# A hint at the head of the program for the branch over a fallback path

## The chip, the cores and the metric

The kernel runs on one core of a Trainium2 chip. A core has a matrix engine (TensorE, PE in the profile; its weight loads are shown as PEld), a vector engine (VectorE, DVE), an activation engine (ScalarE, ACT), a general engine (GpSimd, POOL) and a control engine (SyncE, SP). Each executes its own stream of instructions, in order; the streams meet only at semaphores. DMA queues move data between the device's memory and the core's own memories, and two of the queues in the profile, 8 and 14, move instructions.

The metric is the device time of one execution in microseconds. The time before the change is 607.65 us, the median of three runs (606.86, 607.65 and 607.78).

## The reference

The computation is an attention over normalised queries and keys, followed by a residual two-layer network. For 8 batches, 12 heads, 448 positions and a head width of 64:

```python
q_n, k_n = rmsnorm(q, g_q), rmsnorm(k, g_k)
scores = scale * np.matmul(q_n, k_n.transpose(0, 1, 3, 2))
scores = scores - np.max(scores, axis=-1, keepdims=True)
attn = np.exp(scores)
attn = attn / (np.sum(attn, axis=-1, keepdims=True) + 1e-09)
attn_out = np.matmul(attn, v)

x = attn_out.transpose(0, 2, 1, 3).reshape(8, 448, 768)
xn = (x - mean(x)) / np.sqrt(var(x) + 1e-06) * g_ln
out = x + np.maximum(xn @ w_ch1, 0.0) @ w_ch2
```

The weights w_ch1 and w_ch2 are 768 x 3072 and 3072 x 768. Inputs and output are 32-bit floats in the device's memory.

## The kernel before

The kernel has two versions of the whole computation. The fast one takes shortcuts: the exponential takes a constant offset (EXP_BIAS) in place of each row's maximum, and matmuls run in 16-bit floats. The general one, `_general`, takes the maximum of every row and goes through the batches in a loop, for inputs on which the shortcuts would lose accuracy. The fast version runs always. A test at its end decides whether the general one runs after it and overwrites the output. With the inputs measured here it does not run.

The fast version first does the attention of batch 0, in an order of work written out by hand (the table ORDER). Then `run_rest` walks through the batches. For each it lays out the network's work in chunks (`mlp_chunks`: 24 "up" chunks of six matmuls with 512 columns, L652, and then "down" chunks of six matmuls, L668), and between them it puts the steps of the next batch's attention. For the last batch nothing is left to put between: `run_rest` emits its chunks one after the other, and after the third it calls `flag`. The last down chunks are those of the fourth token tile, and the last 384 columns of that tile are done as two groups of 192. After each group VectorE adds the residual (L672), and `store` sends the rows out (L712), one half on SyncE's queue and one on ScalarE's.

The order is manual on all engines but VectorE in this second part; VectorE's order there is set by the framework's scheduler.

`flag` counts on VectorE how many of the recorded quantities lie inside safe bounds, sums over partitions with one matmul, and writes 0 or 1 to a one-element tile. Then, in the main function, `values_load` (L935) loads that element into a register of every engine (TENSOR_LOAD in the profile), and `tc.If` (L936) becomes one compare-and-branch on every engine:

```python
    val = nc.values_load(sh.flag[0:1, 0:1], min_val=0, max_val=1)
    with tc.If(val > 0):
        _general(tc, sh, q, k, v, g_q, g_k, out)
```

In the built program, the instructions of the general path lie right behind the branch, on each engine, and the end of the program lies behind them. With the flag at 0 every engine jumps over the general path. That path has 1,809 instructions on TensorE, 438 on VectorE, 156 on SyncE, 141 on ScalarE and 26 on GpSimd. Ahead of the branch and with it, the fast version has 9,046 on TensorE, 802 on VectorE, 395 on SyncE, 835 on ScalarE and 335 on GpSimd.

Behind the jump stand a few instructions that the profile puts at L936 too: ScalarE, TensorE and VectorE wait for their own last work, and SyncE waits, one semaphore after the other, for the eight semaphores of its and ScalarE's output stores. Then, at the line of the program's end (L963), SyncE waits twelve times more, for the other queues and the other engines, and all engines meet in two barriers that GpSimd leads.

## Time and profile before

| | before |
|---|---|
| median of three runs | 607.65 us (606.86 to 607.78) |
| the profiled execution | 606.57 us |
| its span, first instruction to last | 604.8 us |
| granted TensorE clock over the span | 0.999 of full speed |
| TensorE busy | 575.8 us, 95% of the span |
| the chain that ended last, TensorE's share | 88% of the span |
| last evacuation on VectorE | 598.45 us, 0.42 us long |
| last stores issued, SyncE and ScalarE | 598.90 us |
| time to landing of these two | 2.2 and 3.1 us |
| branch (L936): TensorE, VectorE, SyncE, ScalarE, GpSimd | 597.4, 599.1, 599.4, 600.5, 540.6 us |
| code moved: queue 8, queue 14 | 37 packets, 0.61 MB; 24 packets, 0.20 MB |

Times in the profile count from the span's first instruction. A group of the profile is written as line, engine, operation, what it writes <- what it reads, count, and durations in ns. An engine's name with a q (SPq, PEldq) stands for the engine's sequencer: register, branch and semaphore instructions and the issue of DMAs, which are not counted as busy. The wait of an instruction that waits for a semaphore lies ahead of the start that is recorded.

### The profile page before, as it was taken

How to read it: one execution, taken by the hardware profiler on the slowest of the kernel's cores; microseconds unless marked ns; L12 is line 12 of the kernel's file. 1: busy time of each engine (PE TensorE's matmuls, PEld its weight loads, DVE VectorE, ACT ScalarE, POOL GpSimd, SP SyncE). 2: the span in 40 equal slices, each digit the busy share in tenths (PEclk: the TensorE clock that was granted, in tenths of full speed). 3: DMA queues.
4: the chain of work that ended last, by engine and by line, in shares of the span. 5: the costliest groups of instructions: out<-in, count | busy, mean ns of one | idle time of the engine just before them, and what ended most of it. 6: DMA issues, size and time to landing. Idle time of an engine off the chain costs nothing.

```text
span 604.8 us, 11485 instructions
## 1 busy us (share of the span) xinstructions
PE 575.8 (95%) x4500; PEld 340.3 (56%) x4500; DVE 287.3 (48%) x643; ACT 358.4 (59%) x673; POOL 184.0 (30%) x245
## 2 busy tenths in 40 slices
PE   2887999999999999999999999999999999999995
PEld 1555666655565666654566666654566666654564
DVE  5899567734356256714256255734256322530011
ACT  5996887368843697448754498538755387124200
POOL 2853432233541355332542345424412000000000
PEclk9999999999999999999999999999999999999999
DMA  8998999484966487948856486948724330130011
GB/s 229 272 198 198 218 226 190 94 175 122 150 140 133 106 111 158 179 123 97 130 140 125 96 118 156 191 114 124 140 58 84 79 62 1 37 95 0 1 53 57
DMA packets 130861, 75.29 MB, mean 124 GB/s; under 512 B 96656, under 2 KB 121040, under 8 KB 130800
## 3 DMA queue, kind: packets, MB, share of 16 engines
q1 hardware_dynamic: 114048, 45.12, 38.4%
q0 software_dynamic: 16080, 28.94, 22.5%
q8 instruction: 37, 0.61, 0.4%
q10 hardware_dynamic: 672, 0.43, 0.2%
q14 instruction: 24, 0.20, 0.1%
HBM read 52.36 MB, written 11.01 MB: 105 GB/s over the span
## 4 chain that ended last, share of the span: by engine, by line
PE 88%; ACT 2%; DVE 2%; issue 0%; DVEq 0%
PE psC L668 36%; PE psH L652 35%; PE psS L353 8%; PE oA L408 5%; PE oB L410 2%; PE psS L359 1%; ACT E L371 1%; PE tr L316 0%; ACT khl L215 0%; PE psU L698 0%; DVE stat L576 0%; ACT hT L654 0%; PE tr L330 0%; DVE xn L597 0%; DVE x L425 0%
## 5 line engine op out<-in xcount | busy, mean ns | idle before, releaser
L652 PE MATMUL psH<-xnT,w 128*128 128x512 f16 (+1 forms) x1134 | 242.0, 353 | 0.0
L668 PE MATMUL psC<-w,hT 128*128 128x384 f16 (+1 forms) x1368 | 234.8, 323 | 0.0
L371 ACT ACTIVATE E<-psS,rr_all 128x448 f16<-128x448 f32 x312 | 193.4, 635 | 48.7 <-PE psS L353 47.8
L654 ACT ACTIVATE hT<-psH 128x512 f16<-128x512 f32 (+1 forms) x189 | 104.0, 550 | 132.2 <-PE psH L652 130.9
L668 PEld LDWEIGHTS <-hT 128*128 128x128 f16 x1368 | 127.2, 98 | 78.8 <-issue 4.3
L652 PEld LDWEIGHTS <-w 128*128 128x128 f16 x1134 | 102.4, 98 | 83.3 <-issue 2.9
L353 PE MATMUL psS<-qU,kU 128*128 128x448 f16 x288 | 101.0, 357 | 8.6 <-ACT E L371 5.7
L408 PEld LDWEIGHTS <-E 128*128 128x128 f16 x936 | 64.5, 98 | 44.5 <-issue 5.1
L229 POOL TENSOR_TENSOR qkv<-qkv,gprod 128x896 f32<-128x896 f32 x21 | 43.6, 2078 | 92.5 <-ACT khl L215 41.1
L408 PE MATMUL oA<-v,E 128*128 128x65 f16 x864 | 66.6, 194 | 0.1
L672 DVE SCALAR_TENSOR_TENSOR x<-psC,rs_all,x 128x384 f32<-128x384 f32 x48 | 29.2, 616 | 78.5 <-PE psC L668 78.1
L128 POOL DMA_DIRECT2D qkv<-in_k_dram x14 | 11.2, 796 | 137.7 <-ACT E L371 82.5
L410 PE MATMUL oB<-v,E 128*128 128x65 f16 x288 | 51.9, 194 | 0.1
L423 DVE RECIPROCAL rec_all<-oA 128x6 f32<-128x6 f32 x48 | 9.3, 194 | 88.1 <-PE oA L408 87.6
L218 DVE TENSOR_REDUCE ssq<-khl 128x14 f32<-128x896 f32 (+1 forms) x24 | 25.6, 1065 | 44.6 <-ACT khl L215 44.5
L353 PEld LDWEIGHTS <-kU 128*128 128x128 f16 x288 | 28.1, 98 | 25.7 <-issue 5.8
L218 DVE TENSOR_REDUCE ssq<-qn 128x14 f32<-128x896 f32 (+1 forms) x25 | 26.1, 1046 | 21.9 <-ACT qn L215 21.8
L68 DVE SCALAR_TENSOR_TENSOR qn<-qkv,rr_all 128x256 f16<-128x256 f32 (+1 forms) x72 | 26.4, 425 | 18.1 <-ACT rr_all L222 18.1
L410 PEld LDWEIGHTS <-E 128*128 128x128 f16 x312 | 30.2, 97 | 0.2 <-DVE xl L430 0.2
L425 DVE TENSOR_TENSOR x<-oA,rec_all 128x384 f32<-128x384 f32 x48 | 26.8, 558 | 1.5
L576 DVE BATCH_NORM_STATS2 stat<-x 128x6 f32<-128x256 f32 (+1 forms) x75 | 26.0, 404 | 0.6
L240 DVE TENSOR_TENSOR khl<-qkv,khl 128x896 f16<-128x896 f32 x21 | 22.7, 1079 | 4.0 <-ACT khl L237 3.9
(111 smaller groups left out, 443.1 us busy)
## 6 DMA issues: line engine op xcount, KB each, us to landing
out_dram<-x SPq DMA_DIRECT2D x20, 384.0 KB, 2.5
qkv<-in_k_dram POOLq DMA_DIRECT2D x14, 384.0 KB, 3.8
qkv<-in_q_dram POOLq DMA_DIRECT2D x14, 384.0 KB, 5.5
qkv<-in_v_dram POOLq DMA_DIRECT2D x14, 384.0 KB, 7.2
w<-in_moe_w_ch_dram POOLq DMA_DIRECT2D x3, 1536.0 KB, 13.0
w<-in_moe_w_ch_dram POOLq DMA_DIRECT2D x2, 2304.0 KB, 22.8
qkv<-in_k_dram SPq DMA_DIRECT2D x7, 384.0 KB, 6.1
qkv<-in_q_dram SPq DMA_DIRECT2D x7, 384.0 KB, 5.7
```

The source lines that it names most:

```text
L68: nc.vector.scalar_tensor_tensor(out=out, in0=x, scalar=8.0, in1=r.unsqueeze(2).broadcast_to([x.shape[0], g, D]), op0=ALU.mult, op1=ALU.mult)
L218: nc.vector.tensor_reduce(out=c["ssq"][:, n], in_=c["sq", n], axis=AX.X, op=ALU.add)
L229: (nc.vector if u in DVE_KG else nc.gpsimd).tensor_tensor(out=c["t"][1], in0=c["t"][1], in1=sh.gprod.unsqueeze(1).broadcast_to([128, g, D] ...
L353: nc.tensor.matmul(ps[0][:, 0:S], c["main"][:, ts(i, 128)], c["q"][:, ts(h, S)], start=True, stop=True)
L371: nc.scalar.activation(out=o, in_=x[:, 0:S], func=AFT.Exp, scale=self.units[u][3][:, g:g + 1], bias=EXP_BIAS)
L408: nc.tensor.matmul(oA[:, t, cs], E[:, ts(t, 128)], rhs, start=(i == 0 and t == 0), stop=(i == 6 and t == 2))
L410: nc.tensor.matmul(oB[:, cs], E[:, 320:448], rhs, start=(i == 0), stop=(i == 6))
L425: nc.vector.tensor_tensor(out=x[:, :, 128 * hp:128 * hp + 128].rearrange("p t (e d) -> p t e d", e=2), in0=oA[:, :, :, 0:D], in1=rec[:, 0: ...
L652: nc.tensor.matmul(ps[:, 0:N], sh.w1[:, dc, ts(f, 128)], xnT[:, dc, 0:N], start=(dc == 0), stop=(dc == NDC - 1))
L654: nc.scalar.activation(out=hT[:, f, 0:N], in_=ps[:, 0:N], func=AFT.Relu)
L668: nc.tensor.matmul(ps[:, 0:g[1]], hT[:, f, ts(t, 128)], sh.w2[:, f, cols], start=(f == 0), stop=(f == NFF - 1))
L672: nc.vector.scalar_tensor_tensor(out=x[:, cols], in0=ps[:, 0:g[1]], scalar=self.rs[:, b, t:t + 1], in1=x[:, cols], op0=ALU.mult, op1=ALU.add)
```

## The change

`If` is given a label, and `run_rest` marks a place for a branch hint with that label, for all five engines, with the hint "LikelyTaken":

```diff
@@ -734,6 +734,8 @@
             total = sum(c for c, _ in chunks)
             if b + 1 == B:
                 for i, (_, emit) in enumerate(chunks):
+                    if i == len(chunks) - 40:
+                        self.tc.mark_branch_hint_location("general", "LikelyTaken", [ENG.PE, ENG.DVE, ENG.SP, ENG.Activation, ENG.Pool])
                     emit()
                     if i == 2:
                         self.flag()
@@ -933,7 +935,7 @@
             fast.run_rest()
 
     val = nc.values_load(sh.flag[0:1, 0:1], min_val=0, max_val=1)
-    with tc.If(val > 0):
+    with tc.If(val > 0, label="general"):
         _general(tc, sh, q, k, v, g_q, g_k, out)
```

In the program as built, this gives one more instruction on each engine, a BranchPrefetchHint that is tied to that engine's compare-and-branch at L936. It does not stand 40 chunks ahead of the end, where the call is. It stands at the head: it is the first instruction that each engine has behind the entry branch of the program, ahead of the first loads. Everything else is the same and in the same order, one place later. (The general path's loop has hints of its own for its back edge, in both versions; they lie inside the path that is jumped over.)

## The prediction

> **What bounds the kernel now.** I read the profile in this order: the page's busy table, the table of three stretches for the end, the groups of the branch's line and of the end's line, the waits of SyncE's queue, and the DMA queues of the last 6 us. From the page:

> ```profile
> span 604.8 us, 11485 instructions
> ...
> PE 575.8 (95%) x4500; PEld 340.3 (56%) x4500; DVE 287.3 (48%) x643; ACT 358.4 (59%) x673; POOL 184.0 (30%) x245
> ...
> q8 instruction: 37, 0.61, 0.4%
> ...
> q14 instruction: 24, 0.20, 0.1%
> ```

> TensorE is the bound for nearly the whole span, and the change takes no matmul away. The two last lines are code being loaded: 37 packets of 16 KB on queue 8 and 24 of 8 KB on queue 14. Up to 598.7 us it is 35 and 19 packets (the last stretch's seven are shown below). TensorE has 9,046 instructions up to the branch: 9,046 / 35, some 256 to a line of code; the other four engines have 2,367 together: 2,367 / 19, some 128 to a line. In the trace each line is fetched as the one before it is entered. What the change can touch is the end. The stretches:

> ```profile
> core 0: us, PE busy (x) PEld busy (x) DVE busy (x) ACT busy (x) POOL busy (x), PEclk, DMA share, GB/s
> ...
> 590.00:598.87 8.87, 8.41 (x76) 6.44 (x74) 2.07 (x4) 0.00 (x0) 0.00 (x0) 1.00 0.24 79
> 598.87:604.80 5.93, 0.00 (x0) 0.00 (x0) 0.00 (x0) 0.00 (x0) 0.00 (x0) 0.88 0.12 29
> ```

> After the last evacuation, at 598.87, 5.93 us go by in which no engine computes. What lies there is shown by the groups of the branch's line (L936, in the stretch from 598 on), then the first two groups of the kernel's closing line (L963):

> ```profile
> L936 SPq EVENT_SEMAPHORE  x8: 17/17/17, 602.6 to 603.1; - x8
> L936 PEldq COMPARE_BRANCH  x1: 4102/4102/4102, 597.4 to 597.4; - x1
> L936 DVEq COMPARE_BRANCH  x1: 72/72/72, 599.1 to 599.1; - x1
> L936 SPq COMPARE_BRANCH  x1: 58/58/58, 599.4 to 599.4; - x1
> L936 ACTq COMPARE_BRANCH  x1: 54/54/54, 600.5 to 600.5; - x1
> L936 ACTq EVENT_SEMAPHORE  x1: 17/17/17, 601.0 to 601.0; - x1
> L936 PEldq EVENT_SEMAPHORE  x1: 51/51/51, 601.5 to 601.5; - x1
> L936 DVEq EVENT_SEMAPHORE  x1: 21/21/21, 602.4 to 602.4; - x1
> ```

> ```profile
> L963 SPq EVENT_SEMAPHORE  x14: 17/28/28, 603.2 to 604.7; - x14
> L963 POOLq EVENT_SEMAPHORE  x4: 17/17/17, 604.0 to 604.7; - x4
> ```

> Compare each engine's branch with its first instruction behind it: TensorE 597.4 to 601.5 (the branch itself lasts 4.1 us), VectorE 599.1 to 602.4, SyncE 599.4 to 602.6, but ScalarE 600.5 to 601.0 only. The distances explain this. The general path that is jumped over has 1,809 instructions on TensorE, 438 on VectorE and 156 on SyncE, more than a line; 141 on ScalarE, which had entered a new line a few instructions earlier and so had the next one; 26 on GpSimd, inside one line. Engines whose target was not loaded stood some 3.1 to 4.1 us; the waits of SyncE's queue have it as a wait for nothing but itself:

> ```profile
> SPq L936 <- SPq L936: 3.1, 1, 3.1
> ```

> The DMA queues from 598.7 on, with the last two stores:

> ```profile
> q14 instruction: 5, 0.04, 2.5%
> q8 instruction: 2, 0.03, 2.4%
> ...
> out_dram<-xl SPq DMA_DIRECT2D x1, 48.0 KB, 2.2
> out_dram<-xl ACTq DMA_DIRECT2D x1, 48.0 KB, 3.1
> ```

> Seven lines of code are fetched here, while the last stores land, at 598.9 + 2.2 = 601.1 (SyncE's) and 598.9 + 3.1 = 602.0 (ScalarE's).

> **The change part by part.** *The five instructions at the head.* No row shows a hint. The nearest are SyncE's four MOVEs at the head, 29 to 42 ns each and some 0.06 us apart (0.0 to 0.2 us); the dearest sequencer step of the trace is a FUSED_REGOPS of 187 ns. All engines take theirs at the same time, just ahead of the first loads at 0.75 us, which ScalarE awaits (2.5 us at its first square), so it passes to the end once: 0 to 0.19 us, taken as 0.06, the MOVE being nearest. It could be free where the first loads have slack, which the wait on them excludes in the main. All later code moves on by one place in its lines, which costs nothing as long as lines are fetched one ahead, as now; where that cover goes, a line's end costs a miss (rival 2).

> *The branch, if the hint has the target's line loaded.* TensorE, VectorE and SyncE would go through as ScalarE does now, 0.4 to 0.5 us from branch to next instruction. On TensorE and VectorE that lies beside SyncE's end: what SyncE waits for from them is asked only in its closing waits (603.2 on), and by then both would have been ready since about 600. On SyncE the path is this: branch at 599.4, next instruction at 599.9 in place of 602.6, and there the eight waits of L936 (now 0.077 us apart, 602.6 to 603.1) stand for the output stores. The first is for SyncE's own last store, the eighth for ScalarE's. So the stall of 3.1 us does not go whole: the stores are late next. First wait through at 601.1, the next seven at 0.077 us: 601.7; the eighth not before ScalarE's store, 602.0. The eighth stands at 603.1 now, so the gain is 603.1 - 602.0 = 1.1 us if the stores land as they did, and 603.1 - 601.7 = 1.4 us if ScalarE's lands in 2.1 us, as the one before it on that queue did (its row has 2.1 us, SyncE's 1.9). With 1.9 us for SyncE's too (600.8, and 0.54 of waits: 601.3) it is 1.8 us. All that follows the eighth wait (1.7 us to the span's end) moves along unchanged.

> Which of these? In the trace the last four data packets of ScalarE's store start at 601.03, as VectorE's fetch of its target ends; all its others had started by 600.64. With the target loaded earlier that fetch is gone, but each engine that enters the new line fetches the one after it some 0.6 us later, so SyncE's, VectorE's and TensorE's next fetches move to 599.5 to 600.6, into the stores' time. I take 1.35 us, close to the middle value, with 1.1 and 1.8 as ends.

> Sum: -1.35 + 0.06 = -1.3 us. The profiled execution took 606.57 us, 1.8 us outside its span, and lies 1.1 us below the median of the runs shown, 607.65 (606.86 to 607.78). The tail is the same work in every execution, so the change is taken off the median: 607.65 - 1.3 = 606.35 us, 0.21% less.

> **The rivals.** *1. Nothing happens at the branch.* The hint stands some 9,000 TensorE instructions ahead of its branch, and what it arms may be lost by then, or the loader may go on line by line. The branch's built form names the general path as its "true" side and the jump over it as its "false" side; if "taken" meant the true side, the line announced would be the next one anyway. For it: all 54 code fetches up to 598.7 us come one line after the other, and no row shows any other pattern. Against it: the same records show that only one branch per engine is executed and that the jump over is what costs a fetch, so it is the taken side. The time is the head's cost alone: 607.65 + 0.06 = 607.7 us. [...]

> *2. The hint fetches at once, and is slower.* If the instruction loads the target's line when it is executed, at 0.75 us, that line takes the place of the line which comes next, and each engine misses at its first line's end: TensorE near 26.4 us, ScalarE and VectorE near 33.6 and 34.9, SyncE near 57, as the first fetches of the trace show. A miss costs what the branch's does, 3.1 to 4.1 us. ScalarE and VectorE are the busiest there (13.55 and 14.28 us of the 15 from 30 to 45), so theirs falls on the path; 1.3 us apart they overlap: some 3.2 us, up to 7.4 if TensorE's 4.1 adds up. [...] It decides as soon as any engine of the head stands more than 1.3 us at its first line's end. For it: it is the plainest reading of a prefetch instruction, and it is placed as early as can be. Against it: nothing in the trace. [...]

> **How the numbers follow.** Hint kept until the branch's line: 0.64. [...] Rival 1: 0.14. Rival 2: 0.22. The bound of what can be told is 0.2%, 1.2 us, which the likeliest case just passes: it gives 1.0 to 1.7 us net, of which I put 0.62 beyond 1.2. Faster: 0.64 x 0.62 = 0.40. Same: 0.24 + 0.14 = 0.38. Slower: 0.22. The likeliest case's own range is 605.8 to 606.7. The stated range starts at 605.5 (runs vary by 0.4 us about their median) and reaches over rival 1 to 608.9, where a mild form of rival 2 begins; about 0.2 is left out.

> **What would show it.** Right: TensorE's, VectorE's and SyncE's first instructions of L936 behind the branch come within 0.5 us of it; SyncE's eight waits start near 601.1 and end by 602.0; the last 6 us have four code fetches in place of seven; the idle end shrinks from 5.93 to about 4.6 us; nothing differs ahead of 590 us by more than 0.1 us. Rival 1: the end is as now. Rival 2: a gap of some 3 us on ScalarE and VectorE between 30 and 36 us, and the end as now. Wrong as to size: the stores land later than 602.0 because code fetches press on them, or SyncE waits behind the branch for something else than the stores.

## The result, and the profile after

The changed kernel takes 605.68 us, the median of 15 runs (605.13 to 607.03), against 607.16 us for 15 runs of the kernel before (606.66 to 608.21). The ratio is 0.9975, with a 95% interval of 0.9968 to 0.9983: 0.25% faster, 1.5 us. The profiled execution took 605.31 us, its span 603.4 us. From its page and from its table of stretches:

```profile
span 603.4 us, 11490 instructions
...
PE 575.7 (95%) x4500; PEld 340.2 (56%) x4500; DVE 287.3 (48%) x643; ACT 358.8 (59%) x673; POOL 183.8 (30%) x245
...
q8 instruction: 36, 0.59, 0.4%
...
q14 instruction: 21, 0.17, 0.1%
```

```profile
590.00:599.14 9.14, 8.69 (x78) 6.63 (x75) 2.07 (x4) 0.00 (x0) 0.00 (x0) 1.00 0.23 77
599.14:603.43 4.29, 0.00 (x0) 0.00 (x0) 0.00 (x1) 0.00 (x0) 0.00 (x0) 1.00 0.10 29
```

No engine's work has changed. The stretch without work behind the last evacuation is 4.29 us long, where it was 5.93 us: 1.64 us less. The last evacuation itself ends 0.27 us later, at 599.14. Where the 1.64 us come from is in the groups of the branch's line, which is L938 now:

```profile
L938 SPq EVENT_SEMAPHORE  x8: 17/17/17, 601.2 to 601.7; - x8
L938 PEldq COMPARE_BRANCH  x1: 393/393/393, 597.7 to 597.7; - x1
L938 PEldq EVENT_SEMAPHORE  x1: 51/51/51, 598.7 to 598.7; - x1
L938 DVEq COMPARE_BRANCH  x1: 84/84/84, 599.4 to 599.4; - x1
L938 SPq COMPARE_BRANCH  x1: 78/78/78, 599.7 to 599.7; - x1
L938 DVEq EVENT_SEMAPHORE  x1: 21/21/21, 600.0 to 600.0; - x1
L938 ACTq COMPARE_BRANCH  x1: 73/73/73, 600.7 to 600.7; - x1
L938 ACTq EVENT_SEMAPHORE  x1: 17/17/17, 601.2 to 601.2; - x1
```

Read each engine's branch against its first instruction behind it, as before. TensorE's branch lasts 0.39 us in place of 4.10. VectorE goes from 599.4 to 600.0, where it stood 3.3 us. SyncE branches at 599.7, and its first wait is through at 601.2. The waits of SyncE's queue still show a wait at this place, but a shorter one, and the code and the stores of the end, from 598.7 on, tell what it is for:

```profile
SPq L938 <- SPq L938: 1.4, 1, 1.4
```

```profile
q14 instruction: 3, 0.02, 1.2%
q8 instruction: 1, 0.02, 1.0%
...
out_dram<-xl SPq DMA_DIRECT2D x1, 48.0 KB, 2.0
out_dram<-xl ACTq DMA_DIRECT2D x1, 48.0 KB, 2.2
```

SyncE's last store was issued at 599.17 and landed 2.0 us later, at 601.2, which is when the first wait is through. So the new wait is for the store. Four lines of code are fetched in this time where there were seven. That is three fewer, as many as there were engines that missed, and they are nowhere extra. Up to 598.7 us the two code queues moved, before and then with the change:

```profile
q8 instruction: 35, 0.57, 0.4%
...
q14 instruction: 19, 0.16, 0.1%
```

```profile
q8 instruction: 35, 0.57, 0.4%
...
q14 instruction: 18, 0.15, 0.1%
```

The hints are the new rows of the closing line's groups, one per engine:

```profile
L965 POOLq BRANCH_PREFETCH_HINT  x1: 56/56/56, 0.7 to 0.7; - x1
L965 ACTq BRANCH_PREFETCH_HINT  x1: 54/54/54, 0.7 to 0.7; - x1
L965 SPq BRANCH_PREFETCH_HINT  x1: 56/56/56, 0.7 to 0.7; - x1
L965 DVEq BRANCH_PREFETCH_HINT  x1: 51/51/51, 0.8 to 0.8; - x1
L965 PEldq BRANCH_PREFETCH_HINT  x1: 50/50/50, 0.8 to 0.8; - x1
```

They put off the first load on ScalarE's queue from 0.75 to 0.82 us, and that on SyncE's from 0.75 to 0.85 us.

### The profile page after: what moved, and what is told of

It reads as the page before. It is cut to its first block, busy times and chain, and to the rows that moved or that the text cites. A ratio compares the mean times of both kernels' runs of the same rounds, so it can differ in the third digit from the quotient of the medians.

```text
span 603.4 us, 11490 instructions
## 1 busy us (share of the span) xinstructions
PE 575.7 (95%) x4500; PEld 340.2 (56%) x4500; DVE 287.3 (48%) x643; ACT 358.8 (59%) x673; POOL 183.8 (30%) x245
## 4 chain that ended last, share of the span: by engine, by line
PE 87%; ACT 2%; DVE 2%; DMA 1%; issue 0%; DVEq 0%
PE psC L668 36%; PE psH L652 34%; PE psS L353 8%; PE oA L408 5%; PE oB L410 2%; PE psS L359 1%; DMA kU<-khl 1%; ACT E L371 1%; PE tr L316 0%; ACT khl L215 0%; PE psU L698 0%; DVE stat L576 0%; DVE xn L597 0%; PE tr L330 0%; ACT hT L654 0%
## 5 line engine op out<-in xcount | busy, mean ns | idle before, releaser
L672 DVE SCALAR_TENSOR_TENSOR x<-psC,rs_all,x 128x384 f32<-128x384 f32 x48 | 29.2, 616 | 78.5 <-PE psC L668 78.1
L68 DVE SCALAR_TENSOR_TENSOR qn<-qkv,rr_all 128x256 f16<-128x256 f32 (+1 forms) x72 | 26.4, 425 | 18.1 <-ACT rr_all L222 18.1
```

The source lines that it names most:

```text
L68: nc.vector.scalar_tensor_tensor(out=out, in0=x, scalar=8.0, in1=r.unsqueeze(2).broadcast_to([x.shape[0], g, D]), op0=ALU.mult, op1=ALU.mult)
L672: nc.vector.scalar_tensor_tensor(out=x[:, cols], in0=ps[:, 0:g[1]], scalar=self.rs[:, b, t:t + 1], in1=x[:, cols], op0=ALU.mult, op1=ALU.add)
```

## The experiments

The theory was that SyncE's missing line of code set the end, and that behind it the landing of the last stores is late next. The rivals were that TensorE's miss, the longest, was the bound; that the gain comes from code fetches which no longer press on the stores; and that the end behind the branch is a fixed series of waits. A second question came up on the way: what the hints cost at the head.

Each edit below is against the changed kernel. In this table "end" is the time from the end of the last evacuation (L672) to the end of the span, taken from the exact times (5.94 us before, 5.93 in the rounded stretch above), and "last evacuation" is when that ends, both of the one profiled execution; the ratio is that of the timed runs to the kernel before.

| kernel | ratio (95% interval) | end, us | last evacuation, us |
|---|---|---|---|
| before | 1 | 5.94 | 598.87 |
| the change | 0.9975 (0.9968 to 0.9983) | 4.29 | 599.14 |
| the change again | 0.9976 (0.9967 to 0.9985) | 4.64 | 600.11 |
| SyncE alone | 0.9991 (0.9982 to 1.0000) | 4.80 | 598.95 |
| all but SyncE | 1.0015 (1.0006 to 1.0024) | 6.08 | 600.09 |
| SyncE and VectorE | 0.9980 (0.9971 to 0.9989) | 4.24 | 599.40 |
| TensorE and VectorE | 0.9997 (0.9988 to 1.0006) | 5.96 | 600.50 |
| SyncE, VectorE, TensorE | 0.9972 (0.9962 to 0.9983) | 4.39 | 599.94 |
| twenty hints each | 0.9993 (0.9984 to 1.0002) | 4.51 | 600.23 |
| two more on ScalarE | 0.9987 (0.9978 to 0.9996) | 4.16 | 601.65 |
| without the last store | 0.9936 (0.9919 to 0.9953) | 2.07 | 599.78 |
| waits in landing order | 0.9981 (0.9969 to 0.9992) | 3.94 | 600.44 |
| three hints, landing order | 0.9968 (0.9957 to 0.9979) | 4.02 | 599.18 |
| the same, small loads first | 0.9994 (0.9985 to 1.0004) | 4.06 | 601.25 |

### Which engine's miss counts

SyncE alone:

```diff
-self.tc.mark_branch_hint_location("general", "LikelyTaken", [ENG.PE, ENG.DVE, ENG.SP, ENG.Activation, ENG.Pool])
+self.tc.mark_branch_hint_location("general", "LikelyTaken", [ENG.SP])
```

> The hint on SyncE alone. Theory (SyncE's missing code line is the end's bound, the stores' landing is late next): SyncE goes from branch to next instruction without the 3.1 us, its eight waits end near 601.7 to 602.0. TensorE and VectorE still miss; VectorE is done at 602.4 to 602.5, which is asked for at SyncE's tenth closing wait only, so 1.1 to 1.4 us of the 1.5 us of the change remain: ratio to before 0.9977 to 0.9982. Rival A (the gain comes from code fetches that no longer press on the last stores, or from the one place by which all code moves): with four engines as before, at most a third of the gain, 0.9992 to 1.000. Rival B (TensorE's 4.1 us, the longest, was the bound): no gain, 1.000.

The end shrank to 4.80 us, 1.14 us of the 1.65 us, as expected of the theory. The timed ratio of 0.9991 was a smaller gain than expected, 0.5 us of 1.5; its interval, 0.9982 to 1.0000, reaches from the expected gain to none. The groups of L938 in its profile:

```profile
L938 SPq EVENT_SEMAPHORE  x8: 17/17/17, 601.4 to 602.1; - x8
L938 PEldq COMPARE_BRANCH  x1: 4242/4242/4242, 597.5 to 597.5; - x1
L938 DVEq COMPARE_BRANCH  x1: 72/72/72, 599.2 to 599.2; - x1
L938 SPq COMPARE_BRANCH  x1: 77/77/77, 599.5 to 599.5; - x1
...
L938 DVEq EVENT_SEMAPHORE  x1: 21/21/21, 602.4 to 602.4; - x1
```

TensorE still stands 4.2 us and VectorE 3.2 us, and SyncE goes on as soon as its store has landed (issued at 598.98, landed 2.4 us later). Here the hint acted on its own engine alone. SyncE now stands twice among its eight waits, and the landing of the last stores tells for what:

```profile
SPq L938 <- SPq L938: 2.0, 2, 1.8
```

```profile
out_dram<-xl SPq DMA_DIRECT2D x1, 48.0 KB, 2.4
out_dram<-xl ACTq DMA_DIRECT2D x1, 48.0 KB, 3.1
```

ScalarE's last store takes 3.1 us to land again, so the eighth wait is through at 602.1 only. That is the whole of what the end lacks. The second reason that was expected, that SyncE's closing waits meet VectorE, did not come about: the closing wait for VectorE is through at 602.68, 0.24 us after VectorE was ready (602.44), the twelve closing waits stand nowhere, and the end behind the eighth wait is as long as before, 1.70 us.

All but SyncE:

```diff
+self.tc.mark_branch_hint_location("general", "LikelyTaken", [ENG.PE, ENG.DVE, ENG.Activation, ENG.Pool])
```

> The hint on the four other engines, none on SyncE. Theory: SyncE's eight waits stay at 602.6 to 603.1 and nothing is gained; with 0.06 us of the head, ratio 0.9998 to 1.0005. Rival A: the fetches of TensorE and VectorE are gone from the last stores' time and the code is moved on four engines, so most of the gain is there: 0.9975 to 0.998. Rival B: 0.9975.

```profile
L938 SPq EVENT_SEMAPHORE  x8: 17/17/17, 603.9 to 604.5; - x8
...
L938 PEldq EVENT_SEMAPHORE  x1: 51/51/51, 599.7 to 599.7; - x1
...
L938 SPq COMPARE_BRANCH  x1: 58/58/58, 600.6 to 600.6; - x1
L938 DVEq EVENT_SEMAPHORE  x1: 21/21/21, 600.9 to 600.9; - x1
```

TensorE and VectorE are through by 600.9 and nothing is gained: SyncE stands 3.3 us, and the end is 6.08 us. TensorE's miss as the bound falls, and so do the code fetches as the main cause. But the time is 0.15% more than before, of which the end explains 0.14 us of 0.9 us; that is taken up below.

SyncE and VectorE (the list of engines is `[ENG.SP, ENG.DVE]`):

> The hint on SyncE and VectorE. Theory: TensorE's miss ends at 601.5, well ahead of SyncE's eleventh closing wait, so the whole gain is there, as with all five: ratio 0.9972 to 0.9979. Rival B: no gain, 1.000.

```profile
L938 PEldq COMPARE_BRANCH  x1: 3818/3818/3818, 597.9 to 597.9; - x1
```

```profile
out_dram<-xl ACTq DMA_DIRECT2D x1, 48.0 KB, 2.2
```

The end is 4.24 us with TensorE still standing 3.8 us at its branch (timed ratio 0.9980, at the edge of what was expected). These two hints give the whole of the end's gain. VectorE's hint brings the 0.5 us that SyncE's alone lacked, by way of the store: with VectorE's miss gone, ScalarE's last store lands in 2.2 us in place of 3.1. So a part of the rival with the code fetches is true: 1.14 us of the 1.65 us are SyncE's stall, and 0.5 us a store that VectorE's fetch no longer holds up.

### What is late next

The last pair of stores is left out, all else as in the change:

```diff
-                if t == n - 1:
+                if t == n - 1 and not (b == B - 1 and cols.start == 576):
```

> As the change, but the last pair of stores (last 192 columns of the last 64-row tiles) is left out, so that part of the output is not written. Theory (behind the branch SyncE stands for the landing of the last stores): SyncE branches some 1.5 us earlier, finds the stores before landed by 599.3, and its eight waits end near 599.8; the closing waits then meet VectorE at 600.0, and the span ends near 601.5, 1.9 us below the change's 603.4: ratio to before 0.994 to 0.9955. Rival (the end behind the branch is a fixed series of waits and barriers, not the landing): the end keeps its 2.2 us behind SyncE's first wait but starts no earlier than the other engines allow; ratio 0.997 to 0.9975.

The end is 2.07 us, 2.2 us less than the change's; ratio 0.9936. The eight waits are spread over the landing of the stores before: the first five go by at 598.9 to 599.2, and the sixth, for ScalarE's store of 597.84, at 600.0, 2.2 us after its issue.

```profile
L938 SPq EVENT_SEMAPHORE  x8: 17/17/17, 598.9 to 600.2; - x8
L938 PEldq COMPARE_BRANCH  x1: 393/393/393, 598.3 to 598.3; - x1
L938 SPq COMPARE_BRANCH  x1: 77/77/77, 598.3 to 598.3; - x1
```

So the landing is what SyncE stands for, and with a hint, work that ends earlier is passed on. The rival of a fixed series falls for the eight waits. It holds for what is behind them: from the start of the eighth wait to the end of the span it takes 1.70 us in each of the fourteen profiles.

In the next kernel the stores of the last batch's three full tiles are cut into pieces, which moves the stores' semaphores on by seven, so that the last store is waited for last:

```diff
+        if t < 3 and b == B - 1:
+            w = DM // (3, 3, 4)[t]
+            for c in range(0, DM, w):
+                nc.sync.dma_start(out[b, 0:384].rearrange("(p j) d -> p j d", j=3)[:, t, c:c + w],
+                                  x[:, c:c + w])
```

> As the change, with the last batch's three full stores cut into 3, 3 and 4 column pieces, which moves the semaphores on by seven: SyncE's last store then is the eighth of its eight waits and ScalarE's the seventh, in place of first and eighth. The same work and bytes. Theory: six of the waits, 0.077 us each, go by before the landing; behind it stand one or two. With landings after 2.0 and 2.2 us as in the change's profile the eighth wait starts 0.3 us earlier: ratio to before 0.9968 to 0.9972, 0.3 us below the change; nothing if ScalarE's store takes 3.1 us again. Rival (order does not matter, each wait is taken when its turn comes after a fixed time): as the change, 0.9975.

The end is 3.94 us, 0.35 us less than the change's, as expected. In the profile six waits go by from 601.53 to 601.93, and the last two at 602.62 and 602.68, 2.1 us after ScalarE's store. The timed ratio of 0.9981 doesn't show it: it lies above both the expected 0.9970 and the change's 0.9975, and its interval holds both.

### What the head costs

Twenty hints on each engine in place of one:

```diff
+                        for _ in range(20):
+                            self.tc.mark_branch_hint_location(...)
```

(The arguments, left out here, are the change's.)

> Twenty hints per engine at the head in place of one, all for the same branch. A hint's row is 50 to 56 ns and it put the first loads off by 0.07 to 0.10 us (0.75 to 0.82 and 0.85). If the head's delay passes to the end whole, 19 more cost 19 x 0.07 = 1.3 us up to 1.9 us: ratio 0.9997 to 1.0007. If the head has slack: 0.9975 as with one. The end of the program should look as with one hint.

The first loads start at 1.92 us on ScalarE's queue and 2.21 us on SyncE's, 1.10 and 1.36 us later than with one hint. In this profile the first matmul starts at 10.46 us, 1.12 us later than in the change's (9.34), and from there to the last evacuation both take 589.8 us. The ratio is 0.9993, 0.0018 above the change's: 1.1 us for 19 hints, 0.06 us each, a little below the range expected for a delay that passes whole. By the two intervals together a hint costs 0.02 to 0.1 us. The head has no slack for it.

Then the 0.15% that all hints but SyncE's lost. There, SyncE's first load came at 0.74 us, ahead of ScalarE's at 0.82 us, and ScalarE's is the one that the first computation waits for. Three kernels were to tell whether that order matters: hints on the three engines that miss, so that ScalarE's load comes first; two more hints on ScalarE, so that it comes last (0.94 against 0.85 us); and hints on TensorE and VectorE alone, so that both start at 0.75 us.

> The hint only on the three engines whose target is not loaded (SyncE, VectorE, TensorE). Theory of the end: as with five. Theory of the head (ScalarE's first loads are the ones that the first computation waits for, and a hint on ScalarE puts them behind SyncE's): ScalarE's first load is issued at 0.75 again, ahead of SyncE's, and the first square starts no later than with five hints: ratio to before 0.9970 to 0.9978, not above the change's 0.9975. If the head's differences are only chance: the same 0.9975.

> All five hints as in the change and two more on ScalarE, which put its first loads behind SyncE's by some 0.1 us. Theory of the head (what made the run without SyncE's hint 0.15% slower than before is that SyncE's loads came ahead of ScalarE's): the first square starts near 7.7 us in place of 6.8, and with the end as in the change the ratio to before is 0.9985 to 0.9995. If the order of the two queues does not matter: 0.1 to 0.2 us behind the change, 0.9976 to 0.9979.

> The hint on TensorE and VectorE alone. Theory of the end: SyncE still misses, the end stays at 6.0 us. Theory of the head (the run with all but SyncE was slower since ScalarE's first load came behind SyncE's): here both start at 0.75 as before the change, so the 0.15% is gone: ratio 0.9995 to 1.0005. Rival (removing the misses on TensorE and VectorE makes SyncE's end later by itself): 1.001 to 1.002 again.

The times came out as expected of the order: 0.9972, 0.9987 and 0.9997. With SyncE's load ahead, two kernels lose some 0.6 to 0.8 us more than their ends and hints explain; with ScalarE's ahead or level, the change and most versions of it do not. Two speak against the order: the kernel with reordered waits and that with SyncE's hint alone lost some 0.7 and 0.5 us in the same way, with ScalarE's load ahead. Each of these losses is hardly larger than the 0.5 to 0.7 us by which its ratio is uncertain. The profiles don't settle it. The first square starts at 7.70 us with all but SyncE, but also at 7.60 us with the three hints, where ScalarE's load came first, and at 7.98 us in the kernel with reordered waits; with two more hints on ScalarE it starts at 7.48 us. In the wait view it stands for the load, in the change by

```profile
ACT hT L215 <- DMA hT<-in_k_dram: 2.7, 1, 2.7
```

and with all but SyncE's hint by

```profile
ACT hT L215 <- DMA hT<-in_k_dram: 3.4, 1, 3.4
```

but one execution of each is too little to tell the order from chance. In the one profile with all but SyncE's hint the loss is at the head: its first matmul comes 1.19 us later than in the kernel before (10.26 against 9.07 us), and from there to the last evacuation both take 589.8 us. In the one with two more hints on ScalarE most of it is not: the first matmul is 0.70 us later than in the change, and another 1.8 us come behind it, 1.0 us near 23 us, where the granted clock is 0.50 for 3.4 us, and 0.8 us near 108 us, where ScalarE stands 1.0 us for a DMA. The order fits three timings and fails two; whether it is a cause stays open.

### A version that does better

Three hints and the waits in landing order, put together, beside the change once more and a version that also issues the two small loads of the first pair ahead of the large one:

```diff
-            main(eng, n, 0)
             left(eng, n, 0, 1)
+            main(eng, n, 0)
```

> The changed kernel once more, for direct comparison with the two versions below on the same chip: ratio to before 0.997 to 0.998, an end of 4.2 to 4.5 us behind the last evacuation.

> The hint on the three engines that miss, and SyncE's last store moved to the eighth of its waits (as in the run before, by cutting the last batch's full stores). Theory: the end of 3.9 us, 0.35 us below the change's, and ScalarE's first load at 0.75 us: ratio to before 0.9965 to 0.9973, 0 to 0.6 us below the change. If the head's differences are chance, 0.9969 to 0.9972.

> As the one before, and on SyncE's and ScalarE's queues the two small loads of the first pair (64 rows each) are issued ahead of the large one (128 rows), in place of behind it. The first square waits for the last of ScalarE's three, the second small one, which lands 4.6 us after its issue where the large one takes 3.3. If the third place in the queue is what is slow, the large one is as late there, and nothing is gained: 0.9965 to 0.9975. If the small ones are slow by themselves (64 partitions with rows of 256 bytes), the first square starts near 5.6 us in place of 6.5 to 6.8 and the ratio is 0.995 to 0.996.

The change repeated its ratio, 0.9976, with an end of 4.64 us, longer than expected (its stores took 2.4 and 2.5 us to land). The granted clock does not explain the gain: on this chip the runs with a clock of 0.999 or more have medians of 607.29 us before (17 runs) and 605.42 us with the change (7 runs). The version with three hints and reordered waits has 0.9968 (0.9957 to 0.9979), 605.45 us against 606.22 us for the change and 607.45 us for the kernel before on the same chip. Its eight waits:

```profile
L943 SPq EVENT_SEMAPHORE  x8: 17/17/17, 600.3 to 601.5; - x8
```

It is clearly faster than the kernel before, and by its median faster than the change, whose interval overlaps with its own. What the reordering adds to the three hints can't be told from the times (0.9968 against 0.9972).

The small loads first were a miss: 0.9994, no gain over the kernel before. The first square started at 6.73 us, no earlier than in the change, and the first matmul at 11.42 us in place of 9.34. From there to the last evacuation it takes the same 589.8 us, so the loss is at the head: here the large load in the third place cost 2.08 us more up to the first matmul than the small one there.

## Why the prediction was right

It said 606.35 us from a median of 607.65, a gain of 1.3 us or 0.21%. Measured were 1.5 us, 0.25%, and the time is within the stated range. It is 0.67 us below the forecast and just below the likeliest case's own range of 605.8 to 606.7: 0.49 us of this is the base, since the kernel before has a median of 607.16 us over fifteen runs, and the other 0.2 us the gain. That the hint is kept was a guess with a chance of 0.64, seen in no row; all in all the prediction gave "faster" 0.40 and "same" 0.38. That the guess came true is in part luck. What the hint is worth once it is kept was worked out from rows, and that held.

- *That a hint at the head is kept until the branch's line.* Right. The three engines that missed go through, and no fetch at the head or at the first lines' ends costs anything. The rival "fetches at once" falls with the profile: no fetch of code starts between 0.2 and 24 us in any of the fourteen profiles, and from 30 to 36 us ScalarE is busy for 5.72 us and VectorE for 5.75 us, as before. The stated range reaches to 608.9 us for a mild form of that rival; no run shows such a cost: the ratios lie between 0.9936 and 1.0015. The rival "nothing happens" falls with the branch rows: 0.39 us in place of 4.10 on TensorE.
- *That only SyncE's stall lies on the path.* Right, by the runs with SyncE alone (end 4.80 us) and with all but SyncE (6.08 us). VectorE's stall did not set the end even with SyncE's gone; its fetch cost 0.5 us there through ScalarE's store.
- *That the landing of the stores is late next, so that 3.1 us of stall give 1.1 to 1.8 us.* Right; with SyncE's hint alone, where ScalarE's store landed in 3.1 us as before, the end lost 1.14 us, the lower case. With the change the eighth wait came 1.6 us earlier against the last evacuation, between the middle case of 1.4 us, in which ScalarE's store lands in 2.1 us, and the upper one of 1.8 us. 1.35 us was taken, below the middle, since the next lines' fetches were thought to press on the stores in turn. That term was too small by 0.3 us: the stores landed in 2.0 and 2.2 us, and the eighth wait came seven waits behind the landing of SyncE's.
- *That VectorE's fetch held up ScalarE's last store.* This was read from one row, and thirteen profiles bear it out: the store took 3.1 us before the change and with SyncE's hint alone, the two kernels in which VectorE misses, and 2.1 to 2.5 us in the eleven profiles in which VectorE has its hint and the store is made. With SyncE's hint alone, too, the store's last four data packets start (601.06) as the fetch that began 1.28 us behind VectorE's branch ends (601.07). Why the packets wait for the fetch is not shown.
- *That a hint costs 0.06 us at the head, in full.* Right as to its row, 50 to 56 ns; the time with twenty gives the same 0.06 us, but only to within 0.02 to 0.1.
- *That nothing ahead of 590 us differs by more than 0.1 us.* Wrong as a reading of single profiles. In this one the last evacuation is 0.27 us late, and over the fourteen it ends between 598.87 and 601.65 us.
- *Three readings on the way.* Seven lines of code are fetched from 598.7 us on, but not all "while the last stores land": four fetches start by 601.6 us, the other three from 602.3 on, when both stores have landed. The dearest sequencer step is not the FUSED_REGOPS of 187 ns (a TENSOR_LOAD takes 473 to 959), so the upper end of 0.19 us for a hint had no ground, though it held. And the sign "within 0.5 us of the branch" was met nearly: VectorE took 0.6 us, TensorE 1.1 us; the last matmul, which TensorE's instruction there waits for, ends 0.04 us before it, at 598.69.

## What to carry to other kernels

In these profiles a taken branch to code that was not loaded cost 3.1 to 4.2 us on each engine that missed, and it is seen as a long branch (TensorE, 4.10 us) or as an empty space behind a short one (VectorE, 3.3 us); compare the engines, because one whose target was near shows the price without a miss (ScalarE, 0.5 us). Count only the engine on which the end waits, and ask what it will meet once it is early: here some 1.5 us of 3.1 us went to the landing of the last stores. A hint per engine cost some 0.06 us here, where the head had no slack, so give it to the engines that miss; the times of three hints and of five (0.9972 and 0.9975) can't tell the difference.

## What the runs showed of the hardware that was not expected

A hint tied to a branch some 9,000 TensorE instructions away still acted (0.39 us at the branch in place of 4.10), and it acted without any fetch more: up to 598.7 us there were 35 packets on queue 8 with it and without, which fits a target loaded in the place of the next line. A store of ScalarE landed 0.9 us later while a line of code was fetched for VectorE (3.1 us against 2.2). And ahead of the end, the executions differ in a few places only. The first is the start: the first square of ScalarE starts between 6.37 and 7.98 us over the fourteen profiles, and mostly the same difference is still there at the first matmul. From the first matmul to the last evacuation ten profiles take the same 589.8 to 589.9 us. The other four take 0.8 to 1.8 us more, near 23 us (in two of them the granted clock is 0.50 there for 3.4 us) and near 108 us, where ScalarE stands 0.9 to 1.0 us for a DMA in three of them.
